# Issuing two DMA transposes ahead of the weight loads at the start of a GEGLU feed-forward kernel

## The chip, the cores and the metric

The program runs on one NeuronCore of a Trainium2 chip. The metric is device time of one execution in microseconds (us). Times vary between executions of one kernel, so every experiment was timed in rounds together with the kernel before, on the same chip (chip 4 for the first and third set of experiments, chip 1 for the second).

## The reference

```python
B, S, D, F = 1, 2048, 1024, 3584          # all bf16
def reference(x, w_gate, w_up, w_down):
    return (gelu_tanh(x @ w_gate) * (x @ w_up)) @ w_down
```

## The kernel before

The kernel works on S in two halves. Nearly all of it runs Strassen-like block products (lines 379 and 615 in the profile); these form the steady part. Before the steady part can start, the first 512 tokens and the first chunk of weights (512 columns of gate and up) are worked through plainly, by line 245. Only this start is touched here.

TensorE needs x transposed, D on the partitions, in eight blocks of 128. Blocks 0 to 3 of the first 512 tokens are loaded plainly and transposed on TensorE (line 295). Blocks 4 to 7 come as DMA transposes (line 172). Weights come for the same eight blocks of D: first the columns 0 to 255 of the chunk, in pieces of rows, then the "other columns" 256 to 511.

```python
def load_w(key, j, k0, k1, queue=sp, f0=0, f1=FG):   # j: 0 gate, 1 up
    eng = nc.scalar if queue is act else nc.sync
    queue(eng.dma_start(out=chunks[key][j][:, k0:k1, f0:f1], in_=...))   # cut
def load_xT(xT, h, tb, k0, k1):                      # always on SyncE
    sp(nc.sync.dma_start_transpose(out=xT[:, k0:k1, ...], in_=...))      # cut

load_x0(0, sp)                         # blocks 0,1 of x, 256 KB
load_w(first, 0, 0, 2, act, 0, FA)     # FA = 256 columns
load_w(first, 1, 0, 2, sp, 0, FA)
load_x0(1, act)                        # blocks 2,3 of x, 256 KB
load_w(first, 0, 2, 4, sp, 0, FA)
load_w(first, 1, 2, 4, act, 0, FA)
act(nc.scalar.preload_act_table(ACT.Gelu_apprx_tanh))
# ... eight warm-up matmuls on constants (line 197) ...
for j in range(2):
    load_w(first, j, KH, KD, sp, 0, FA)              # KH = 4, KD = 8
for j in range(2):
    for kd in (KH + 2 * j, KH + 2 * j + 1):
        load_xT(xT, 0, 0, kd, kd + 1)
    load_w(first, j, 0, KD, sp, FA, FG)              # other columns, 512 KB each
for k0 in range(0, KD, KH):
    load_xT(xT, 0, 1, k0, k0 + KH)                   # the next 512 tokens

def first_units(hT):                                 # order of the matmuls
    transpose_x0(0)
    order = [(0, 0), (0, 1), (1, 0), (1, 1)]         # (gate/up, block)
    order += [(j, kd) for kd in range(2, KD) for j in range(2)]
    for j, kd in order:
        for u in range(2):
            mm_gu(banks[held[u][j]], (wg, wu)[j], u, 0, kd)
        if (j, kd) == (1, 0):
            transpose_x0(1)
```

## Time and profile before

| | before |
|---|---|
| time, median of the first 3 runs (all 6 of the first comparison) | 543.43 us (543.65 us) |
| span of the profiled run | 541.3 us |
| TensorE busy | 534.5 us, 99% |
| waits of TensorE on a transfer, whole kernel | one, 0.55 us, at block 6 |
| steady part (line 379) starts | 34.28 us |

In the profile a line gives start and duration in us, engine, source line, operation and destination <- source; the brackets at the end hold the idle time ahead of it and what ended it. "SPq" and "ACTq" are the queues from which SyncE and ScalarE issue DMAs: there a duration is the time taken to issue and not the transfer. In the waits view a line reads: who waited, on whom, us in total, times, longest. A load "lands" when its completion is signalled to the engines.

One derived number serves for all versions. From the first matmul after the second group of TensorE transposes (up of block 1) to the start of the steady part there are always 122 matmuls. In the changed kernel's first profile they run without a break in 26.36 us. In any other run, that stretch less 26.36 us is what TensorE lost there. It counts waits that the idle time understates, because matmuls overlap. For the kernel before, two lines of its TensorE timeline give it, the row at 7.22 that the prediction shows and this one:

```profile
34.28 1.89 PE L379 MATMUL bank<-xT,w_mem 128*128 128x512 bf16 x8
```

34.28 - 7.22 - 26.36 = 0.70 us lost.

### The profile page before, as it was taken

What the parts mean: (1) busy time and instruction counts of PE and PEld (TensorE: products, weight loads), DVE (VectorE), ACT (ScalarE), POOL (GpSimd) and SP (SyncE); (2) the same over time, 40 slices, a digit from 0 to 9 for tenths busy, and PEclk for the clock granted to TensorE, in tenths of its full rate; (3) what the DMA queues carried; (4) which work ended last, traced back from release to release, by engine and by line L of the source; (5) the groups of instructions that cost most, each with busy time, mean ns of one, the idle gap of its engine ahead of it and who ended that gap; (6) DMA issues with size and microseconds to landing.
All of it is one profiled execution on the core that took longest, in us unless ns stands there. A gap on an engine that the chain in (4) does not pass through costs nothing.

```text
span 541.3 us, 7194 instructions
## 1 busy us (share of the span) xinstructions
PE 534.5 (99%) x2356; PEld 373.1 (69%) x2392; DVE 350.6 (65%) x465; ACT 258.4 (48%) x433; POOL 239.7 (44%) x206
## 2 busy tenths in 40 slices
PE   8999999999999999999999999999999999999997
PEld 4457777776677676767777767777667776866865
DVE  0746666787765999889574444444454469979961
ACT  1435555555555319216455555555555552452270
POOL 0197777888777000000057766677777630000000
PEclk9999999999999999999999999999999999999999
DMA  9956598988836979789952240404040457777946
GB/s 226 306 169 144 183 262 251 173 291 165 278 121 224 347 260 335 217 268 304 311 202 92 64 142 14 156 1 156 0 155 1 157 166 247 249 221 246 289 146 206
DMA packets 85924, 104.80 MB, mean 194 GB/s; under 512 B 18816, under 2 KB 67456, under 8 KB 85888
## 3 DMA queue, kind: packets, MB, share of 16 engines
q1 hardware_dynamic: 84816, 103.83, 62.3%
q10 hardware_dynamic: 1072, 0.52, 0.4%
q8 instruction: 19, 0.31, 0.2%
q14 instruction: 17, 0.14, 0.1%
HBM read 87.03 MB, written 13.63 MB: 186 GB/s over the span
## 4 chain that ended last, share of the span: by engine, by line
PE 97%; DMA 1%; SPq 1%; issue 0%; ACT 0%; ACTq 0%
PE bank L379 60%; PE bank L615 32%; PE bank L245 4%; DMA xT<-in_x_dram 1%; DMA w_mem<-in_w_gate_dram 1%; SPq L172 0%; ACT o_sb L663 0%; SPq L161 0%; ACTq L663 0%
## 5 line engine op out<-in xcount | busy, mean ns | idle before, releaser
L379 PE MATMUL bank<-t_mem,s_mem 128*128 128x512 f32 x1016 | 249.2, 399 | 0.0
L379 PEld LDWEIGHTS bank<-t_mem,s_mem 128*128 128x128 f32 x1016 | 190.9, 188 | 44.1
L353 POOL TENSOR_TENSOR s_mem<-w_mem 128x512 fp32r<-128x512 bf16 x100 | 117.1, 1191 | 197.2 <-DMA w_mem<-in_w_up_dram 105.0
L615 PE MATMUL bank<-t_mem,s_mem 128*128 128x512 f32 x560 | 130.2, 392 | 0.0
L402 DVE TENSOR_TENSOR bank<-bank,m 128x512 f32<-128x512 f32 x104 | 72.1, 698 | 82.8 <-ACT bank L422 74.5
L615 PEld LDWEIGHTS bank<-t_mem,s_mem 128*128 128x128 f32 x560 | 105.1, 188 | 22.9 <-issue 0.2
L269 DVE TENSOR_TENSOR hT<-w_mem,bank 128x512 bf16<-128x512 f32 x104 | 71.3, 687 | 59.1 <-ACT w_mem L264 24.2
L264 ACT ACTIVATE w_mem<-bank 128x512 f32<-128x512 f32 x104 | 61.7, 596 | 80.1 <-DVE bank L402 48.0
L379 PE MATMUL bank<-xT,w_mem 128*128 128x512 bf16 x391 | 97.5, 380 | 1.3
L379 PEld LDWEIGHTS <-w_mem 128*128 128x128 bf16 x416 | 36.6, 98 | 50.4 <-issue 13.3
L528 DVE TENSOR_TENSOR t_mem<-w_mem 128x1024 fp32r<-128x1024 bf16 x56 | 65.6, 1217 | 0.0
L353 POOL TENSOR_TENSOR s_mem<-w_mem,s_mem 128x512 fp32r<-128x512 bf16 x50 | 63.5, 1294 | 0.0
L353 POOL TENSOR_TENSOR s_mem<-s_mem,w_mem 128x512 fp32r<-128x512 f32 x50 | 60.7, 1232 | 0.0
L366 ACT CAST s_mem<-w_mem 128x512 fp32r<-128x512 bf16 x52 | 32.0, 616 | 32.4 <-PE bank L379 28.4
L590 DVE TENSOR_TENSOR s_mem<-hT 128x512 fp32r<-128x512 bf16 x56 | 40.5, 755 | 10.5 <-PE bank L615 7.0
L615 PEld LDWEIGHTS <-hT 128*128 128x128 bf16 x224 | 21.3, 98 | 26.6 <-issue 1.8
L417 ACT COPY m<-bank 128x512 f32<-128x512 f32 x52 | 30.6, 589 | 17.1 <-PE bank L379 17.0
L422 ACT COPY bank<-bank 128x512 f32<-128x512 f32 x52 | 29.6, 570 | 17.0 <-PE bank L379 17.0
L413 ACT COPY bank<-bank 128x512 f32<-128x512 f32 x52 | 29.6, 570 | 13.2 <-PE bank L379 13.2
L663 ACT CAST o_sb<-bank 128x512 bf16<-128x512 f32 x28 | 15.4, 585 | 39.6 <-PE bank L615 39.6
L245 PE MATMUL bank<-xT,w_mem 128*128 128x512 bf16 x125 | 28.0, 379 | 0.8 <-DMA xT<-in_x_dram 0.5
L525 ACT CAST t_mem<-w_mem 128x1024 fp32r<-128x1024 bf16 x28 | 26.9, 1047 | 0.0
(39 smaller groups left out, 230.7 us busy)
## 6 DMA issues: line engine op xcount, KB each, us to landing
t_mem<-t_dram SPq DMA_DIRECT2D x56, 512.0 KB, 5.1
w_mem<-in_w_gate_dram SPq DMA_DIRECT2D x11, 1024.0 KB, 6.4
w_mem<-in_w_up_dram SPq DMA_DIRECT2D x11, 1024.0 KB, 8.6
wd_sb<-in_w_down_dram SPq DMA_DIRECT2D x28, 256.0 KB, 3.9
t_dram<-o_sb SPq DMA_DIRECT2D x28, 256.0 KB, 2.8
wd_sb<-in_w_down_dram SPq DMA_DIRECT2D x12, 512.0 KB, 8.7
w_mem<-in_w_down_dram SPq DMA_DIRECT2D x10, 512.0 KB, 6.6
w_mem<-in_w_down_dram SPq DMA_DIRECT2D x4, 1024.0 KB, 6.7
```

What stands on the lines that cost most here:

```text
L245: nc.tensor.matmul(ps[:], lhsT=w_sb[:, kd, fi * P : (fi + 1) * P], rhs=xT[:, kd, tb * TB : (tb + 1) * TB], start=(kd == 0), stop=(kd == KD ...
L264: act(nc.scalar.activation(out=g_sb, in_=ps[:], func=ACT.Gelu_apprx_tanh))
L269: nc.vector.tensor_tensor(out=hT[:, fc, tb * TB : (tb + 1) * TB], in0=g_sb, in1=ps[:], op=ALU.mult,)
L353: pool(nc.gpsimd.tensor_tensor(out=t, in0=in0, in1=in1, op=op))
L366: act(nc.scalar.copy(out=t, in_=a(1, 1)))
L379: nc.tensor.matmul(banks[bank][:], lhsT=lhs[:, c, :], rhs=rhs[:, c, :], start=start and c == 0, stop=c == KH - 1, skip_group_check=True,)
L402: nc.vector.tensor_tensor(out=banks[dst][:], in0=banks[src][:], in1=m5[j][:], op=ALU.add)
L413: act(nc.scalar.copy(out=banks[QB[j]][:], in_=banks[PB[j]][:]))
L417: act(nc.scalar.copy(out=m5[j][:], in_=banks[VB[j]][:]))
L528: dve(nc.vector.tensor_tensor(out=t, in0=in0, in1=in1, op=ALU.subtract))
L590: dve(nc.vector.tensor_tensor(out=t, in0=in0, in1=in1, op=op))
L615: nc.tensor.matmul(banks[bset[u]][:], lhsT=lhs(i, u), rhs=rhs(i), start=start and i == 0, stop=stop and i == NS - 1, skip_group_check=True,)
```

## The change

The intent is to let the queue of SyncE start its slow transposes at once and to have block 6 no longer behind the 512 KB of other gate columns. To make room among the first eight loads, which go out without a semaphore wait (the prediction explains this), the weights of rows 2 to 5 go to ScalarE's queue and those of rows 5 to 8 follow on SyncE's.

```diff
     load_x0(1, act)
-    load_w(first, 0, 2, 4, sp, 0, FA)
-    load_w(first, 1, 2, 4, act, 0, FA)
+    for j in range(2):
+        load_xT(xT, 0, 0, KH + j, KH + j + 1)
+        load_w(first, j, 2, 5, act, 0, FA)
...
     for j in range(2):
-        load_w(first, j, KH, KD, sp, 0, FA)
+        load_w(first, j, 5, KD, sp, 0, FA)
+    for kd in range(KH + 2, KD):
+        load_xT(xT, 0, 0, kd, kd + 1)
     for j in range(2):
-        for kd in (KH + 2 * j, KH + 2 * j + 1):
-            load_xT(xT, 0, 0, kd, kd + 1)
         load_w(first, j, 0, KD, sp, FA, FG)
```

## The prediction

> **What bounds the kernel now.** I read the page first: busy shares, then the chain that ended last.
>
> ```profile
> PE 534.5 (99%) x2356; PEld 373.1 (69%) x2392; DVE 350.6 (65%) x465; ACT 258.4 (48%) x433; POOL 239.7 (44%) x206
> PE 97%; DMA 1%; SPq 1%; issue 0%; ACT 0%; ACTq 0%
> ```
>
> TensorE is busy for 534.5 of 541.3 us and carries 97% of the chain. Of the remaining 3%, most is the start. So the next view was TensorE's own waits, over the whole span:
>
> ```profile
> PE bank L197 <- PEq L896: 0.8, 1, 0.8
> PE bank L245 <- DMA xT<-in_x_dram: 0.5, 1, 0.5
> ```
>
> The first is the launch. The second is the only time in the whole kernel that a matmul stands behind a transfer, and it is what the change aims at. The change touches nothing but the order and size of loads in the first 20 us, so its direct gain is bounded by that one wait. The timeline of TensorE shows where it lies:
>
> ```profile
> 6.78 0.61 PE L295 MATMUL bank<-ident,w_mem 128*128 128x128 bf16 x8
> 7.22 4.07 PE L245 MATMUL bank<-xT,w_mem 128*128 128x512 bf16 x18
> 11.84 2.54 PE L245 MATMUL bank<-xT,w_mem 128*128 128x512 bf16 x10 [0.55 <-DMA xT<-in_x_dram]
> ```
>
> The 18 matmuls from 7.22 us are up of block 1, then gate and up of blocks 2 to 5 of D, two matmuls each. What stops is block 6. The idle time shown is 0.55 us, but the loss is larger, because matmuls overlap: the chain has 49 of them in 10.74 us, one per 0.219 us, while one lasts 0.38. The 18th starts at 11.29 - 0.38 = 10.91; the 19th could start at 10.91 + 0.22 = 11.13 and starts at 11.84. That is 0.71 us.
>
> Why the transpose of block 6 comes so late is in the start of the chain and in the queue of SyncE:
>
> ```profile
> 0.73 3.42 DMA w_mem<-in_w_gate_dram
> 4.17 1.22 SPq L172
> 5.43 1.24 SPq L172
> 6.72 0.58 SPq L161
> 7.34 4.45 DMA xT<-in_x_dram
> ```
>
> ```profile
> SPq L172 <- DMA w_mem<-in_w_gate_dram: 0.8, 1, 0.8
> ```
>
> Each transpose costs the queue 1.2 us (an ordinary load 0.5 to 0.6). The first does not start before 4.17, as it waits 0.8 us for the first weight load to land. That is no data dependence: in the listing of instructions all loads share eight completion semaphores in turn, and the ninth load waits for the first to give its own back. The transposes of blocks 4 and 5 are the ninth and tenth. Then comes a 512 KB load of other weight columns, and only then block 6, issued at 7.34 and landed 4.45 us later at 11.80.
>
> **What the Trainium skill says.** The page "DMA: Bandwidth & Descriptors", section "Issuing engines are not separate DMA queues", says that loads started from several engines run on the same 16 DMA engines, and that a second queue saves only the issuing time. The trace agrees that bytes limit here: the windows below show the rate flat over both phases, with two queues in use up to about 6 us and one after.
>
> ```profile
> 2.00:4.00 2.00, 2.00 (x6) 0.59 (x4) 0.00 (x0) 1.28 (x1) 0.00 (x0) 1.00 0.89 258
> 4.00:6.00 2.00, 1.79 (x12) 1.12 (x12) 0.72 (x2) 0.37 (x1) 0.00 (x0) 1.00 1.18 307
> 6.00:8.00 2.00, 2.00 (x17) 1.14 (x16) 0.42 (x1) 0.58 (x1) 0.00 (x0) 1.00 1.28 275
> 8.00:10.00 2.00, 2.00 (x11) 0.88 (x9) 0.00 (x0) 0.01 (x1) 0.00 (x0) 1.00 1.07 269
> 10.00:11.50 1.50, 1.29 (x6) 0.49 (x5) 0.00 (x0) 0.00 (x0) 0.00 (x0) 1.00 1.30 253
> 11.50:12.00 0.50, 0.16 (x1) 0.10 (x1) 0.00 (x0) 0.00 (x0) 0.00 (x0) 1.00 0.52 63
> ```
>
> (The last two columns are the DMA share and GB/s; the five before the clock are busy us by engine.) The same page, section "Queues, rings and completion order", says that within a queue descriptors are consumed in order, and that each engine alternates between queues that have work. So a transpose put early on SyncE's queue takes turns with ScalarE's loads; the trace of before has no transpose beside a busy second queue, so this is untried here. Section "Silent corruption: two transposing streams in flight at once" forbids transposes from two queues together; the change keeps all on SyncE, so its result should stay right.
>
> **The change part by part.**
> (1) Issue. The eight loads without a semaphore wait now include the transposes of blocks 4 and 5. SyncE issues x (0.74), up 0 to 2 (1.24), then at once transpose 4 at about 1.8 and 5 at about 3.0, done by 4.3, where before they went out at 4.17 and 5.43: 2.4 us earlier.
> (2) Blocks 6 and 7. SyncE then issues gate and up 5 to 8 (their semaphores, of loads that landed at 0.73 + 3.4 = 4.1 and 0.74 + 3.6 = 4.3, are free), to about 5.4. Transpose 6 waits for the second x load's semaphore, landed at 1.24 + 4.5 = 5.7 before, so it goes out at 5.8 to 6.4 instead of 7.34, and transpose 7 about 1.3 us later, where before it was 8.82. The 512 KB load no longer lies ahead of them. With landing times as before (3.4 to 4.6 us), block 6 lands by 9.4 to 11.0; by bytes (2,048 KB from the start through block 7, at about 270 GB/s) near 10. TensorE wants it at 11.13. The 0.71 us go.
> (3) Weights 2 to 5. These are the price. Before, gate 2 to 4 landed at 1.79 + 4.2 = 6.0 and up 2 to 4 at 1.83 + 4.6 = 6.4. Now both are half as large again (192 KB for 128), both sit on ScalarE's queue, up behind gate, and they share the engines with the two transposes. TensorE wants gate 2 at 7.22 + 2 x 0.22 = 7.66 and up 2 at 8.09. Bytes up to the end of up 2 to 5: ScalarE's queue 128 + 256 + 192 + 192 = 768 KB, SyncE's 256 + 128 for x and up, 256 for the transposes, together 1,408 KB or 1,442 thousand bytes. By the windows, 26 + 516 + 614 = 1,156 thousand have moved at 6.00, the rest takes 286 / 275 = 1.04 us: last byte at 7.04. From last byte to landing I take 0.7 us, from block 7's transpose: the rate collapses at 11.5 and it landed at 8.82 + 3.4 = 12.2. So up 2 to 5 lands at 7.75 at best. If SyncE's gate 5 to 8 (192 KB) moves in the same stretch, 197 / 275 = 0.7 us are added: 8.45. Against 8.09 that is a stall between 0 and 0.4 us; I take 0.2, and 0.05 more for transposes moving somewhat fewer bytes per second.
> (4) ScalarE issues one load more (about 0.5 us), so its table load moves from 2.39 to about 2.9 and ends near 4.2; its first copy was at 5.06. Free.
> (5) Later loads. The other columns of gate are issued near 8.3 instead of 6.72, and by bytes (512 KB more after the 2,048) land near 12; TensorE wants them after block 7, at 13.57 before and 12.86 with the gap gone. Those of up go out near 9 instead of 10.12 (landed 14.7) and are wanted at 14.6. Then the transposes of the second token block and the next chunk come over 1 us earlier, with no TensorE wait on them before. Free, with about 0.8 us to spare on the first.
> Sum: -0.71 + 0.25 = -0.46 us of 543.43, so 543.0. After 13 us both kernels run the same program with TensorE never waiting, so what is won at the start is neither lost nor multiplied.
>
> **Rivals.**
> A: the wait moves. The stall on up 2 to 5 is as long as the one removed, because the two queues share unevenly and the transposes crowd out ScalarE's loads. For it: the margin is only 8.09 - 7.75 = 0.34 us at best, and the second x load, on the same queue and wanted at 6.56, would slip too. Against it: the rate is a total, and these bytes are ahead of everything else. It gives 543.4 to 544.0.
> B: full gain. The weights are just in time and all 0.71 us are won: 542.7. For it: gate and up 2 to 5 have fewer bytes ahead of them than the old order put in the same 7 us.
> C: hidden. Block 6 comes earlier but the other columns of gate, issued 1.5 us later, become the next wait. By (5) there are 0.8 us of slack, so I give it one chance in ten; it would leave about 543.3.
> D: no effect that the clock can show, since three runs of before span 543.17 to 544.63, three times the expected gain.
>
> **Range and chances.** The mechanism allows 542.7 to 543.9; the runs' own scatter adds some 0.2 below and, from the lone 544.63, more above, but a median drops a lone outlier. I predict 543.0 with 542.5 to 543.8 for 8 in 10. Two per cent is 10.9 us, fifteen times the whole wait: within 2% is almost certain.
>
> **What would show it.** Step 1: transposes on SyncE at about 1.8 and 3.0, without the 0.8 us semaphore wait. Step 2: no TensorE wait on the transposes at block 6, landing near 10. Step 3: a wait of TensorE on gate or up weights at about 7.7 to 8.1, up to 0.4 us; a longer one is rival A, none is B. Step 5: no wait near 12.9 or 14.6. The start of the steady part (34.45 before, the first matmul of line 379) should come 0.3 to 0.7 us earlier and the span shrink by as much. The prediction is wrong if the start gains nothing, or if it gains and the span does not, which would mean a later coupling that I don't see.

## The result, and the profile after

The changed kernel took 542.96 us (median of 6, 542.49 to 543.76), the kernel before 543.65 us in the same rounds (median of 6). The ratio is 0.9986, 95% interval 0.9974 to 0.9999: within 2%, and inside the predicted range; the interval only just leaves out 1. (Line numbers of the changed kernel are one higher below the edit: 246 for 245, 380 for 379, 616 for 615.)

From the page of the changed kernel, busy TensorE and the chain that ended last:

```profile
PE 536.1 (99%) x2392; PEld 373.0 (69%) x2392; DVE 350.2 (65%) x465; ACT 258.6 (48%) x433; POOL 240.7 (45%) x206
PE 98%; DMA 1%; ACT 0%; issue 0%; ACTq 0%
```

SyncE's queue no longer appears in the chain. TensorE's own waits over the whole span:

```profile
PE bank L198 <- PEq L897: 0.8, 1, 0.8
PE bank L246 <- ACT xT L306: 0.2, 1, 0.2
```

The wait on the transpose is gone, and no transfer keeps a matmul waiting. (The 0.2 us behind ScalarE's copy cost nothing: the matmuls concerned start at 5.47, those of before at 5.49. The busy sum rose by 1.6 us although the kernel got faster: the trace of before lacks 36 matmul records, 2,356 for 2,392.) SyncE's queue shows why:

```profile
1.78 2.51 SPq L172 DMA_TRANSPOSE xT<-in_x_dram  x2
4.34 0.58 SPq L161 DMA_DIRECT2D w_mem<-in_w_gate_dram  x1
4.96 0.49 SPq L161 DMA_DIRECT2D w_mem<-in_w_up_dram  x1
5.54 2.43 SPq L172 DMA_TRANSPOSE xT<-in_x_dram  x2
8.01 0.58 SPq L161 DMA_DIRECT2D w_mem<-in_w_gate_dram  x1
```

Transposes 4 and 5 go out from 1.78 us (4.17 before), 6 at 5.54 (7.34 before); block 6 landed at 9.98 (11.80 before), over a microsecond before it was wanted. The chain ends its first stretch so:

```profile
7.37 26.36 PE bank L246 x122
33.73 6.28 PE bank L380 x28
```

The timeline dates the same stretch 0.16 us earlier, at its start and at its end alike:

```profile
7.21 26.53 PE L246 MATMUL bank<-xT,w_mem 128*128 128x512 bf16 x122
33.57 1.89 PE L380 MATMUL bank<-xT,w_mem 128*128 128x512 bf16 x8
```

That unbroken stretch, 33.57 - 7.21, is where the 26.36 us come from. By the timeline the steady part starts at 33.57, 0.71 us before the 34.28 of before (the prediction's 34.45 is the same start as the chain dates it); the spans, 541.3 and 540.5, differ by 0.8.

So far this is the prediction's rival B, the full gain. But it is one profile, and the same 5.5 us of program in the second experiment below gave a stall that this one lacks. The kernel was therefore measured twice more; that changes the picture.

### The profile page after: what moved, and what is told of

It is laid out like the page before. It is cut to its first block, busy times and chain, and to the rows that moved or that the text cites. A ratio compares the mean times of both kernels' runs of the same rounds, so it can differ in the third digit from the quotient of the medians. Undisturbed runs are those within 1.5% of the kernel's fastest.

```text
span 540.5 us, 7229 instructions
## 1 busy us (share of the span) xinstructions
PE 536.1 (99%) x2392; PEld 373.0 (69%) x2392; DVE 350.2 (65%) x465; ACT 258.6 (48%) x433; POOL 240.7 (45%) x206
## 3 DMA queue, kind: packets, MB, share of 16 engines
HBM read 87.03 MB, written 13.63 MB: 186 GB/s over the span
## 4 chain that ended last, share of the span: by engine, by line
PE 98%; DMA 1%; ACT 0%; issue 0%; ACTq 0%
PE bank L380 61%; PE bank L616 33%; PE bank L246 5%; DMA w_mem<-in_x_dram 1%; PE bank L296 0%; ACT o_sb L664 0%; ACT xT L306 0%; ACTq L664 0%
## 5 line engine op out<-in xcount | busy, mean ns | idle before, releaser
L354 POOL TENSOR_TENSOR s_mem<-w_mem 128x512 fp32r<-128x512 bf16 x100 | 118.7, 1208 | 195.4 <-DVE t_mem L239 103.2
L380 PE MATMUL bank<-xT,w_mem 128*128 128x512 bf16 x416 | 98.8, 380 | 0.0
L246 PE MATMUL bank<-xT,w_mem 128*128 128x512 bf16 x128 | 28.0, 379 | 0.2 <-ACT xT L306 0.2
```

Source lines behind the costliest of these rows:

```text
L246: nc.tensor.matmul(ps[:], lhsT=w_sb[:, kd, fi * P : (fi + 1) * P], rhs=xT[:, kd, tb * TB : (tb + 1) * TB], start=(kd == 0), stop=(kd == KD ...
L354: pool(nc.gpsimd.tensor_tensor(out=t, in0=in0, in1=in1, op=op))
L380: nc.tensor.matmul(banks[bank][:], lhsT=lhs[:, c, :], rhs=rhs[:, c, :], start=start and c == 0, stop=c == KH - 1, skip_group_check=True,)
```

## The experiments

The results in one table. "x landed" is the landing of the first 256 KB of x (of the later of its halves in the last two rows), "up 2" that of the load which holds up's block 2. "Lost" is the stretch described above less 26.36 us; in the last two rows there is loss ahead of that stretch as well. The ratio is to the kernel before in the same rounds.

| version | x landed | up 2 landed | lost, us | what TensorE waited for | steady part starts | median us (runs) | ratio (95%) |
|---|---|---|---|---|---|---|---|
| before | 4.37 | 6.46 | 0.70 | block 6 | 34.28 | 543.65 (6) | 1 |
| changed, first | 4.37 | 7.68 | 0.00 | nothing | 33.57 | 542.96 (6) | 0.9986 (0.9974 to 0.9999) |
| changed, second | 4.31 | 8.50 | 0.45 | up 2 to 5 | 34.03 | 544.23 (6) | 1.0009 (0.9993 to 1.0026) |
| changed, third | 4.63 | 8.96 | 0.78 | up 2 to 5, later other up columns | 34.67 | 543.64 (6) | 0.9994 (0.9981 to 1.0007) |
| order only | 4.41 | 6.55 | 0.95 | other gate columns | 34.62 | 544.15 (4) | 1.0012 (0.9996 to 1.0029) |
| early only | 4.43 | 8.85 | 1.66 | up 2 to 5, then block 6 | 35.09 | 543.68 (4) | 1.0003 (0.9988 to 1.0018) |
| rows 2, 2, 4, first | 4.58 | 7.54 | 0.10 | nothing listed | 33.92 | 542.65 (4) | 0.9985 (0.9970 to 1.0000) |
| rows 2, 2, 4, second | 4.30 | 8.29 | 0.34 | up 4 to 8 | 34.04 | 542.79 (5) | 0.9985 (0.9973 to 0.9997) |
| plain load for T5 | 4.31 | 8.73 | 0.47 | up 2 to 5 | 34.25 | 542.99 (4) | 0.9992 (0.9976 to 1.0009) |
| one queue | 4.62 | 8.14 | 0.78 | other gate columns | 34.40 | 543.52 (4) | 0.9999 (0.9985 to 1.0013) |
| up first, first | 4.71 | 6.74 | 0.00 | nothing | 34.08 | 542.98 (5) | 0.9987 (0.9974 to 0.9999) |
| up first, second | 4.56 | 6.84 | 0.25 | other gate columns | 34.00 | 542.74 (5) | 0.9982 (0.9970 to 0.9994) |
| x halves | 3.96 | 6.16 | 2.28 | a copy on ScalarE, up 5 to 8 | 36.18 | 546.45 (6) | 1.0045 (1.0031 to 1.0059) |
| x halves, mended | 3.93 | 8.71 | 0.97 | next tokens' blocks | 35.43 | 543.45 (6) | 0.9995 (0.9983 to 1.0007) |

My theory (M): the gain needs both halves of the change, block 6 ahead of the 512 KB and the transposes issued early, and its price is the race of the weights 2 to 5 against the transposes. The rivals: the order alone suffices (R1), or the early issue alone (R2).

### Order only

```diff
 # the kernel before
     for j in range(2):
         load_w(first, j, KH, KD, sp, 0, FA)
+    for kd in range(KH, KD):
+        load_xT(xT, 0, 0, kd, kd + 1)
     for j in range(2):
-        for kd in (KH + 2 * j, KH + 2 * j + 1):
-            load_xT(xT, 0, 0, kd, kd + 1)
         load_w(first, j, 0, KD, sp, FA, FG)
```

> The kernel before, with the four single-block transposes kept together ahead of the two 512 KB loads of other weight columns; nothing goes out earlier. Theory M (both halves of the change are needed: block 6 must not lie behind the 512 KB load, and the queue must start its transposes about 2.4 us earlier so that the loads behind them also come in time): transpose 6 is issued at about 6.7 us and lands near 10.3 to 10.8, so the wait at block 6 goes, but the other columns of gate are issued near 9.3 instead of 8.0 and land near 13.3, after the 12.9 at which TensorE wants them: a new wait of 0.3 to 0.6 us there, the steady part starts between 33.9 and 34.3 us (33.73 in the changed kernel, 34.45 before). Rival R1 (only the order before block 6 matters): no wait at all, steady part at 33.7, the whole gain of 0.7 us.

Measured: block 6 landed at 10.07, so the old wait went. The chain of this run shows what came in its place:

```profile
8.05 1.26 SPq L172
9.30 0.04 issue
9.35 4.45 DMA w_mem<-in_w_gate_dram
13.80 0.05 issue
13.85 9.49 PE bank L245 x43
```

The other gate columns are issued only at 9.35, behind four transposes of 1.2 us each, and land at 13.80, about 0.9 us after TensorE could have used them. R1 is refuted: the loss only moves, and it even grew a little (0.95 for 0.70; expected 0.3 to 0.6). In the changed kernel the same load goes out at 8.01. What brings it forward by 1.3 us is the rest of the change, which is two things: the early issue, and the weights taken off SyncE's queue. The one-queue run below tells them apart.

### Early only

```diff
 # the changed kernel
+    load_w(first, 0, 0, KD, sp, FA, FG)
     for kd in range(KH + 2, KD):
         load_xT(xT, 0, 0, kd, kd + 1)
-    for j in range(2):
-        load_w(first, j, 0, KD, sp, FA, FG)
+    load_w(first, 1, 0, KD, sp, FA, FG)
```

> The changed kernel, with the 512 KB load of gate's other columns put back between transposes 5 and 6; the early transposes stay. Theory M: block 6 again lies behind 512 KB, lands at 11.5 to 12.0 us, and TensorE waits 0.3 to 0.8 us for it as before; steady part at 34.1 to 34.5. Rival R2 (the early issue alone is what counts; transpose 6 goes out near 6.2 instead of 7.34, 1.2 us earlier, and lands 1.2 us earlier, at 10.6): no wait, steady part at 33.7.

TensorE's waits in this run, those on transfers:

```profile
PE bank L246 <- DMA xT<-in_x_dram: 0.6, 1, 0.6
PE bank L246 <- DMA w_mem<-in_w_up_dram: 0.5, 1, 0.5
...
PE bank L296 <- DMA w_mem<-in_x_dram: 0.2, 1, 0.2
```

Transpose 6 went out at 6.03 and landed at 12.61, behind the 512 KB (12.01). R2 is refuted; M holds as far as these two runs test it. The landing is later than the 11.5 to 12.0 expected, and the trace shows something else that was not expected: up 2 to 5 landed at 8.85 and held TensorE up at block 2, although up to 5.5 us this program is the changed kernel's, whose profile has that load landing at 7.68.

### The changed kernel again, twice

No edit.

> The changed kernel itself, unedited, because the run with only the early issue showed a stall of 0.5 us at up 2 to 5 with the same first 5.5 us of program in which the changed kernel's profile showed none (up 2 to 5 landed at 8.9 and 7.7). If the landing of ScalarE's second loads beside the transposes scatters from run to run: up 2 to 5 lands again somewhere in 7.6 to 8.9, the steady part starts between 33.7 and 34.5, and the prediction's stall of 0 to 0.4 us was right as a range. If it is fixed by the program: 7.7 again, no wait, steady part at 33.7. The time against before: 0.4 to 0.8 us less.

The chain of the second profile leads through the very load that step 3 of the prediction was worried about:

```profile
1.83 0.53 ACTq L161
2.39 6.12 DMA w_mem<-in_w_up_dram
8.55 25.64 PE bank L246 x118
```

Up 2 to 5 took 6.12 us and landed at 8.50 (7.68 in the first profile). So it scatters; the gain at the start fell to 0.25 us here. (This set ran on another chip than the third, but a difference of chips does not explain the scatter: "rows 2, 2, 4" ran twice on chip 4, and its up 2 landed at 7.54 and 8.29.)

> The changed kernel a third time, because its second measurement (544.2 us, against 543.0 in the first) had a wait of 1.0 us near 272 us, on the last rows of the fourth sum that are read back from memory, which its first profile did not have, and which the run with the order alone, whose start differs otherwise, had too (1.4 us). If that wait is scatter of the memory traffic and no work of the change: some runs show it and some do not, as those of the kernel before beside them, and the ratio to before lies between 0.9975 and 1.0005. If the change causes it: most runs of the changed kernel lie above 544.5 and none of before does. The landing of up 2 to 5: again anywhere in 7.6 to 8.9 us.

The third profile, TensorE's timeline:

```profile
7.53 1.13 PE L246 MATMUL bank<-xT,w_mem 128*128 128x512 bf16 x4
9.00 25.84 PE L246 MATMUL bank<-xT,w_mem 128*128 128x512 bf16 x115 [0.34 <-DMA w_mem<-in_w_up_dram]
```

It landed at 8.96, 6.58 us after its issue, and the loss is 0.78 us, more than the kernel before loses. About 0.6 of it is at block 2, more than the prediction's upper bound of 0.4. The other 0.2 came later: the other up columns landed at 15.62, and the matmul that needs them, due at about 15.49, started at 15.67. The three losses 0.00, 0.45 and 0.78 average 0.41, which leaves 0.29 us of gain against 0.70.

The second set of timed runs was slower than the kernel before, and the start does not explain that. Its waits show another one:

```profile
PE bank L616 <- DMA t_mem<-t_dram: 1.0, 2, 0.5
PE bank L198 <- PEq L897: 0.8, 1, 0.8
PE bank L246 <- DMA w_mem<-in_w_up_dram: 0.3, 1, 0.3
```

At 272 us, in the middle of the kernel, TensorE waits for the last rows of a sum that is read back from memory. In the order-only run the same wait reads:

```profile
PE bank L615 <- DMA t_mem<-t_dram: 1.4, 2, 0.8
```

The slowest of the seven loads between 250 and 275 us landed 7.0 us after issue in the changed kernel's first profile and 7.2 in that of before, without a wait; 7.5 in the third (a wait of 0.2), 8.2 in the second (1.0) and 8.8 in the order-only run (1.4). In the other nine traces it landed 6.2 to 6.8 us after issue, without a wait. The margin is thus a few tenths of a microsecond in the kernel before and in the changed kernel, and the order-only run, which does not have the changed kernel's early issue, is hit hardest. So the wait does not need the changed start. Whether the changed kernel is hit more often stays open. Six of its 18 timed spans are above 542.0 us, four of the 29 of the kernel before in the three sets of experiments, and none of the 19 of the "rows" and "up first" versions below, which share the rest of its program; I have no experiment that tells why.

### Rows 0 to 2, 2 to 4, 4 to 8

```diff
 # the changed kernel
-        load_w(first, j, 2, 5, act, 0, FA)
+        load_w(first, j, 2, 4, act, 0, FA)
-        load_w(first, j, 5, KD, sp, 0, FA)
+        load_w(first, j, 4, KD, sp, 0, FA)
```

> The changed kernel with the weight rows split as before, 0 to 2, 2 to 4, 4 to 8, on the queues of the change. If the split into 2 to 5 and 5 to 8 is needed, up 4 to 8 (256 KB, issued near 5.0 us) lands after the 9.8 at which TensorE wants it, and the wait is 0.2 to 0.6 us. If it is not (my theory, by a margin of about 0.2 us): gate 4 to 8 lands near 8.7 to 9.1 and up 4 to 8 near 9.6, no wait, steady part at 33.7. Beside that: in the changed kernel transpose 5 moved no bytes from 5.5 to 6.9 us, until ScalarE's queue was empty. If it is held by that queue, then with 128 KB less on it transpose 5 lands 0.3 to 0.5 us earlier than its 8.2 us; if it is held by itself, at 8.2 again.

First run: no wait listed, a loss of 0.10 us. The split into 2 to 5 and 5 to 8 is not needed for the gain. Transpose 5 landed at 8.06 (8.24), too small a difference from the expected 0.3 to 0.5, and too much scatter around it, to say what holds it: inconclusive.

> The version with rows 0 to 2, 2 to 4, 4 to 8 a second time (first 542.65 us median of 4). If its smaller loads of rows 2 to 4 make the wait at block 2 rarer than in the changed kernel: up 2 to 4 lands by 8.0 again, no wait at block 2, none or at most 0.1 us at up 4 to 8 (it landed at 9.79 and is wanted at 9.8 to 10.0), and a median of 0.3 us or more under the changed kernel's in the same rounds. If the two splits are worth the same: medians within 0.3 us.

Second run: rows 2 to 4 landed at 8.29, later than the 8.0 expected, and up 4 to 8 at 10.24, in the chain:

```profile
4.96 5.28 DMA w_mem<-in_w_up_dram
10.24 0.05 issue
10.29 1.68 PE bank L246 x7
```

That cost 0.34 us. With 128 KB in each early load the race at block 2 is eased, but a small one opens at block 4. Against the changed kernel of the same rounds the median is 0.85 us lower (542.79 and 543.64), of which the start explains 0.63, the difference of the two steady starts, 34.67 and 34.04. About half of that is not the new split: the first x load landed at 4.63 in the one profile and at 4.30 in the other.

### A plain load in the place of transpose 5

```diff
 # the changed kernel
-    for j in range(2):
-        load_xT(xT, 0, 0, KH + j, KH + j + 1)
-        load_w(first, j, 2, 5, act, 0, FA)
+    load_xT(xT, 0, 0, KH, KH + 1)
+    load_w(first, 0, 2, 5, act, 0, FA)
+    load_w(first, 0, 5, KD, sp, 0, FA)
+    load_w(first, 1, 2, 5, act, 0, FA)
...   # up 5 to 8 and transposes 5 to 7 follow on SyncE's queue
```

> The changed kernel with gate 5 to 8, a plain load of 192 KB, in the place of transpose 5, which moves behind up 5 to 8. It tests the assumption of the prediction's step 3, that the two queues take turns, so that 192 KB on SyncE's queue delay up 2 to 5 (it landed at 7.7 in the changed kernel) by 0.7 us. If plain loads take turns: up 2 to 5 lands at 8.2 to 8.6 and TensorE waits 0.1 to 0.5 us at block 2. If SyncE's queue yields whatever it holds: 7.6 to 7.8, no wait there. Later, the other columns of gate go out near 8.5 and may cost up to 0.4 us at 12.9 in both cases, and transpose 7 is near its limit, so the landing times decide here and not the total.

Up 2 to 5 landed at 8.73, as if the two queues took turns, a little over the expected 8.2 to 8.6. When this run was planned, 7.68 was the only value of the unedited kernel; with its 8.50 and 8.96 known, 8.73 tells nothing. Inconclusive.

### One queue

```diff
 # the changed kernel
-        load_w(first, j, 2, 5, act, 0, FA)
+        load_w(first, j, 2, 5, sp, 0, FA)
```

> The changed kernel with gate and up 2 to 5 taken from ScalarE's queue and put on SyncE's, each behind its transpose. It tests the two queues part of the change. If two queues matter because SyncE's is bound by issuing (1.2 us for each transpose): up 2 to 5 goes out near 4.8 instead of 2.4, lands at 8.2 to 8.9, TensorE waits 0.1 to 0.8 us at block 2, and the other columns of gate go out 1 us later and cost another 0.2 to 0.5: steady part at 34.2 to 34.8, no gain or a loss. If only bytes count (the same total on one queue): up 2 to 5 lands near 7.7 and the steady part starts at 33.7 to 33.9. Beside that, if it is a transpose beside another queue's loads that slows the engines (between 5.0 and 6.5 us the changed kernel moved about 210 to 230 GB/s, against 275 to 300 around it), then with one queue this dip is gone.

```profile
9.07 4.55 DMA w_mem<-in_w_gate_dram
13.67 20.89 PE bank L246 x96
```

The loss is in the issuing: up 2 to 5 went out at 4.88, yet landed at 8.14, in time; the other gate columns went out at 9.07 for 8.01 and landed at 13.63, which cost 0.78 us. That the second queue saves issue time on SyncE's is shown here, and this agrees with the page "DMA: Bandwidth & Descriptors" of the Trainium skill, which the prediction quotes on two queues. (That it saves nothing else, as the page also says, is not shown.)

This corrects M. The run has the order and the early issue and still sends the other gate columns out at 9.07, only 0.28 us before the order-only run; the remaining 1.06 us to 8.01 come from taking weights 2 to 5 off SyncE's queue. So the move of the weights is a third part that the gain needs. What the early issue is worth alone was not run (the new order with weights on ScalarE's queue, but late transposes).

The run also had a second question: is it a transpose beside another queue's loads that lowers the rate between 5.0 and 6.5 us? The window 5.0 to 6.5 of, in this order, the kernel before, the changed kernel's first, second and third run, one queue, and the two runs of the next version (last column GB/s):

```profile
5.00:6.50 1.50, 1.36 (x10) 0.75 (x8) 0.57 (x2) 0.37 (x1) 0.00 (x0) 1.00 1.17 285
```
```profile
5.00:6.50 1.50, 1.26 (x10) 0.64 (x8) 0.56 (x2) 0.37 (x1) 0.00 (x0) 1.00 1.22 219
```
```profile
5.00:6.50 1.50, 1.47 (x9) 0.71 (x8) 0.51 (x2) 0.37 (x1) 0.00 (x0) 1.00 1.23 224
```
```profile
5.00:6.50 1.50, 1.47 (x11) 0.90 (x10) 0.72 (x2) 0.37 (x1) 0.00 (x0) 1.00 1.21 176
```
```profile
5.00:6.50 1.50, 1.26 (x11) 0.69 (x8) 0.70 (x2) 0.37 (x1) 0.00 (x0) 1.00 1.25 239
```
```profile
5.00:6.50 1.50, 1.47 (x11) 0.91 (x9) 0.72 (x2) 0.37 (x1) 0.00 (x0) 1.00 1.21 287
```
```profile
5.00:6.50 1.50, 1.26 (x11) 0.72 (x9) 0.72 (x2) 0.37 (x1) 0.00 (x0) 1.00 1.31 285
```

With one queue the dip is smaller (239) but not gone, so the second queue is at most part of its cause. The kernel before and the next version, which move mostly plain loads in this window, reach 285 to 287. But the dip is not simply that transposes move their bytes slowly. The DMA view of the changed kernel's first profile, 5.5 to 6.5 us (q10 is ScalarE's queue, q1 SyncE's; packets, MB):

```profile
q10 hardware_dynamic: 444, 0.22, 121.0%
q1 hardware_dynamic: 33, 0.00, 2.9%
```

With transposes 4 and 5 both issued, SyncE's queue moved almost nothing (0.00 to 0.01 MB in all three profiles), and ScalarE's plain loads, nearly alone, came to 186 to 222 GB/s. In "up first" the rate falls later, to 216 and 164 GB/s between 6.5 and 7.5 us, while its transposes 4 and 5 move. The mechanism is not settled here.

### Up first: the version that the runs point to

If the race of weights 2 to 5 against the transposes is what takes the gain back, then one of the two should go ahead of them:

```diff
 # the changed kernel
     load_x0(1, act)
-    for j in range(2):
-        load_xT(xT, 0, 0, KH + j, KH + j + 1)
-        load_w(first, j, 2, 5, act, 0, FA)
+    load_w(first, 1, 2, 5, sp, 0, FA)
+    load_w(first, 0, 2, 5, act, 0, FA)
+    for j in range(2):
+        load_xT(xT, 0, 0, KH + j, KH + j + 1)
...
-    for j in range(2):
-        load_w(first, j, 5, KD, sp, 0, FA)
+    load_w(first, 0, 5, KD, sp, 0, FA)
+    load_w(first, 1, 5, KD, act, 0, FA)
```

> The changed kernel, made safer: up 2 to 5 goes out on SyncE's queue ahead of transposes 4 and 5, gate 2 to 5 alone stays on ScalarE's, and up 5 to 8 moves to ScalarE's queue behind its table load. If the weights of blocks 2 to 5 racing the transposes are what can still stall the changed kernel: both land by 6.8, no wait at block 2, transposes 4 and 5 land 0 to 0.8 us later than in the changed kernel but before 9.4 and 10.3 where they are wanted; steady part at 33.7 in every run, and a median 0.1 to 0.3 us under the changed kernel's. If not: the same as the changed kernel, or up 5 to 8 on the second queue becomes a new wait near 10.5.

Up 2 to 5 landed at 6.74 and gate at 7.24 (expected 6.8), transposes 4 and 5 at 7.70 and 8.22. The loss is 0.00. The steady part starts at 34.08 and not at 33.7, because the first x load landed at 4.71 in this run, 0.34 us later than in the changed kernel's first profile, and the first six matmuls took 1.62 us for 1.46.

> The version with up 2 to 5 ahead of the transposes a second time (first 542.98 us median of 5, all between 542.6 and 543.2). Its weights 2 to 5 landed at 6.7 and 7.2, so whatever the memory traffic does they are there before 7.7 and 8.1. I expect no wait of TensorE on transfers before 20 us, apart from the one on the first x load, in this trace either, and a median of 542.8 to 543.2.

Again no wait at block 2 (up landed at 6.84). The expectation of no wait at all missed: the other gate columns landed at 13.22, which cost 0.25 us.

```profile
8.21 5.01 DMA w_mem<-in_w_gate_dram
13.22 0.04 issue
13.27 9.46 PE bank L247 x43
```

Its ten timed runs lie between 542.51 and 543.16; the changed kernel's 18 between 542.47 and 545.45. In the rounds of the second call the medians are 542.98 against 544.23, in those of the third 542.74 against 543.64. Of the three versions measured more than once, it and "rows 2, 2, 4" had a ratio below 1 each time: here by 0.13% and 0.18%, both intervals just below 1. The starts, 34.08 and 34.00 for 34.28, explain only part of these 0.7 and 1.0 us.

### x in halves, and mended

In every version above TensorE starts its real work when the first x load lands, 4.30 to 4.71 us. This version splits that load over both queues, ahead of everything else.

```diff
 # up first
-    NWARM = 8
+    NWARM = 7
-    load_x0(0, sp)
+    load_x0(0, sp, 0, 2)      # first two of the four token tiles
+    load_x0(0, act, 2, 4)
...   # up 5 to 8: on ScalarE's queue, behind the first copy of transposed x
-        load_w(first, j, 0, KD, sp, FA, FG)
+        load_w(first, j, 0, KH, sp, FA, FG)
+        load_w(first, j, KH, KD, sp, FA, FG)
```

> The version before, with the first x load in two halves on the two queues ahead of everything else, seven warm-up matmuls for eight, up 5 to 8 behind ScalarE's first copy, and the other columns of gate and up in two loads each. In the changed kernel TensorE starts its real work at 4.41 us, when the first x load (256 KB) lands, which shares the engines with 128 KB of gate. With x alone in front it should land near 3.95 to 4.05, TensorE start at 4.0 to 4.1, and if everything behind keeps up the steady part start at 33.3 to 33.4, 1.1 us before the kernel before. If the start is bound by bytes all the way (every later load is wanted 0.4 us earlier too), a wait of 0.1 to 0.4 us appears at block 1, 6 or at the other columns, and the steady part starts at 33.5 to 33.8.

x landed at 3.70 and 3.96 as hoped, and the kernel became 2.4 us slower. Two lines of TensorE's timeline:

```profile
4.89 2.37 PE L248 MATMUL bank<-xT,w_mem 128*128 128x512 bf16 x6
...
10.07 2.32 PE L248 MATMUL bank<-xT,w_mem 128*128 128x512 bf16 x10 [0.87 <-ACT xT L308]
```

The first six matmuls took 2.37 us where the other versions need 1.46 to 1.72: they ran at about one per 0.43 us, the pace of the warm-up, until 6.57. The Trainium skill, page "TensorE: Matmul & The Clock Gate", section "Part 1: The HAM clock gate (the "warmup" mystery)", says that TensorE runs at half clock until it was busy through a window of some 3.4 us that does not start with the kernel. This trace agrees in the pace, 0.43 and 0.22 us per matmul. The switch came 1.8 us later here than in the changed kernel's first profile (4.8 us). That seven warm-up matmuls replace eight may be the reason, but it is not shown: with eight the switch scatters as well, from before 4.5 us (early only) to about 6.1 (the first "up first" profile). Second, ScalarE, sent to issue up 5 to 8, waited for a load's semaphore until 8.98 with a copy behind it. My reading of which semaphore it would get was wrong.

Mended: eight warm-up matmuls, up 5 to 8 on SyncE's queue, gate 2 to 5 (not up) ahead of the transposes.

> The version with the first x load in halves, mended: eight warm-up matmuls again (with seven, TensorE's matmuls ran at 0.43 us each until 6.4 us instead of 0.22), up 5 to 8 on SyncE's queue (on ScalarE's it waited for a semaphore and held up a copy for 0.9 us), gate 2 to 5 ahead of the transposes. x landed at 3.7 and 3.96 there; so TensorE starts its transposes at 4.15 to 4.35 in every run, where the other versions scatter from 4.36 to 4.76. If nothing else comes late the steady part starts at 33.3 to 33.6 and the median is 0.1 to 0.4 us under the changed kernel's. If up 2 to 5, last on ScalarE's queue beside the transposes, lands after 8.1 as it did there: a wait of 0.1 to 0.5 us, and no gain over the changed kernel.

```profile
PE bank L249 <- DMA xT<-in_x_dram: 0.8, 1, 0.8
...
PE bank L299 <- DMA w_mem<-in_x_dram: 0.7, 1, 0.7
```

TensorE started at 4.14, and lost more than that later: the second x load landed at 7.60 (5.5 to 5.9 in the versions before "x halves") and the transposes of the next 512 tokens at 22.44 (18.6 to 21.2). It is no faster than the kernel before. To land the first load 0.4 to 0.8 us sooner gains nothing while the later loads are not there sooner too.

## Why the prediction was right, and where not

- **Steps 1 and 2, the issue and blocks 6 and 7: right.** Transposes at 1.78 and 3.04 us, no semaphore wait, block 6 landed at 9.98 ("near 10"). The 0.71 us that the matmul spacing gave for the wait, and not the 0.55 that the waits view lists, is what the first profile won (34.28 to 33.57). Transpose 6 went out at 5.54, ahead of the predicted 5.8 to 6.4, as the second x load, whose semaphore it takes, landed at 5.52 and not 5.7. That the order alone is not enough, that the early issue without it is not, and that the second queue is needed too was not in the prediction; the three experiments show it.
- **Step 3, the stall on up 2 to 5: right in kind, mis-sized.** It was put at 0 to 0.4 us with 0.2, plus 0.05 for the transposes, as the middle. Three profiles gave 0.00, 0.45 and about 0.6; the landing was put at 7.75 to 8.45 and measured 7.68, 8.50 and 8.96. The term that failed is the rate, 275 GB/s for the bytes after 6 us: between 5.0 and 6.5 us the changed kernel moved 176 to 224, and the 0.05 us for transposes was too little. The flat rate that the prediction read from the windows of before did not carry over. The range also took for a fixed quantity what scatters from run to run. That the first landing, 7.68, is close to the predicted best, 7.75, is luck: two errors cancelled. By 6.0 us fewer bytes had moved than assumed (1.07 MB, not 1.16), but the 0.13 MB of transpose 5, which the sum put ahead of up 2 to 5, moved behind it, so that 1.33 MB had moved when its last byte did. In the second and third profile transpose 5's bytes did go ahead, and that total was 1.48 and 1.51 MB (the prediction has 1.44).
- **Step 4, ScalarE's table load: right in effect.** It began at 3.15, not at 2.9, as the fourth issue took 0.73 us; nothing waited for it.
- **Step 5, later loads: no wait in the first profile, but the slack was wrong.** The other gate columns landed at 12.76, not "near 12", with 0.1 us to spare and not 0.8. The other up columns, which were to be free, cost about 0.2 us in the third profile. Rival C itself did not come about in the changed kernel, but at this margin it was nearer than one chance in ten: the order-only and one-queue runs and one "up first" run fall to just this load, by 0.95, 0.78 and 0.25 us.
- **The sum.** Predicted -0.46 us; measured -0.69 between the first medians, and by the mean of the losses in three profiles -0.29. The three ratios, 0.9986, 1.0009 and 0.9994, average 0.9996. The first median's closeness to the predicted 543.0 was luck: the gain was 0.23 us larger than predicted, and the median of before 0.22 us above the 543.43 that it was taken from. Of the three medians 542.96, 543.64 and 544.23, two are inside 542.5 to 543.8. By the prediction's own test, that it is wrong if the start gains nothing, the third profile (a loss of 0.78 for 0.70) counts against it.
- **The last sentence of "Sum", that TensorE never waits after 13 us in either kernel, is wrong as a rule.** The read-back near 272 us cost 0.2 and 1.0 us in two profiles of the changed kernel. Rival D, scatter that hides the effect, was the best description of the totals.

So the answer to "is it faster" is: at its start, by 0.7 us at best and 0.3 on average of three profiles; as a whole kernel, not shown. The versions "up first" (losses 0.00 and 0.25) and "rows 2, 2, 4" (0.10 and 0.34) kept more of it, in two profiles each.

## What to carry to other kernels

When a queue's slow issues (here 1.2 us for a transpose of one block) hold up everything behind them, issue them early and keep large loads that are wanted later behind them; but put what is wanted first ahead of them, since moving one load only passes the wait to the next load that has no slack. List, for each load, when it lands and when it is wanted, and want more than a few tenths of a microsecond between the two. Take more than one profile before a stall that is not in the first one is called absent.

## What the Trainium skill lacked or had wrong

- "DMA: Bandwidth & Descriptors", rules for kernel authors: a transpose next to ordinary DMAs needs nothing. The passage is about correct results, and these runs agree (all were correct). Of speed it says nothing: here the rate from 5.0 to 6.5 us was 176 to 224 GB/s with transposes issued beside ordinary loads, for 285 before, and a 192 KB load on the other queue landed 5.3 to 6.6 us after its issue. The page has a rate for transposes, but none for transposes beside ordinary loads.
- The same page has no time that a DMA transpose of one block (128 by 512) holds its issuing queue on this chip in us, only a count of sequencer cycles for small tiles on earlier generations: 1.12 to 1.26 us in most cases here, where a plain load mostly takes 0.45 to 0.58. This was decisive in the order-only and one-queue runs.
- "TensorE: Matmul & The Clock Gate" puts the switch to full pace at around 4 us of sustained matmuls with 500 ns of scatter (while it also says that the count of slow matmuls varies by more between runs); here, with matmuls from 0.77 us on and short gaps between them, it came between less than 4.5 and about 6.6 us after the start of the span, thus after less than 3.7 to about 5.8 us. The granted clock in the profile read 1.00 while matmuls ran at half pace, so that column does not show it.
- No page tells how much the landing of one load scatters between executions of the same program: 7.68, 8.50 and 8.96 us for up 2 to 5, 4.31 to 4.63 us for the first x load in the three profiles of the changed kernel.
